# Set attention and a gated convolution: x in two host layouts, float32 scores in column strips, row-tiled gates

## The chip, the cores and the metric

One NeuronCore of one Trainium2 chip. The metric is the device time of one execution in microseconds. TensorE multiplies, VectorE (DVE), ScalarE (ACT) and GpSimd (POOL) work on tiles of 128 partitions, SyncE (SP) issues most DMAs; TensorE's results go to PSUM, eight banks of 128 x 512 float32, which GpSimd does not read.

## The reference

Four batches of 12800 tokens with 128 channels, 32 inducing vectors, five convolution taps, cut to what is computed:

```python
def mab(q, kv):
    s = scale * (q @ kv.transpose(0, 2, 1))
    s = s - s.max(-1, keepdims=True)
    a = np.exp(s)
    a /= a.sum(-1, keepdims=True) + 1e-09
    return a @ kv
h = mab(I, x)                 # 32 rows over 12800 tokens of the batch
x = mab(x, h)                 # 12800 rows over 32
xp = np.concatenate([np.zeros((B, K - 1, D)), x], axis=1)
for k in range(K):
    gate_pre += conv_w[k][None, None, :] * xp[:, k:k + S, :]
gate = 1.0 / (1.0 + np.exp(-gate_pre))
return (gate * (x @ w_val)) @ w_out
```

The second attention's output is never formed: with P the 12800 x 32 softmax, x = P h, so gate and value are products of P with h scaled by each tap, and with h w_val. x comes as float32, the weights as float64 bits that the kernel turns into float32 itself.

## The kernel before

**Layout.** A batch lies as 128 partitions of 100 consecutive tokens. Seven chunks of 8, 12 and 5 x 16 token columns (1024 to 2048 tokens) are the unit; six to eight columns, 512 KB at most, the unit of a load.

**Phase 1 of a batch, `sched_a` and `sched_b`.** `load` brings x on SP's queue. `split1` (L188, ScalarE) and `split2` (L200, VectorE) split it into two float16 halves x1 and x2. These are turned channel-first into xT, by `trans_dma` (L206, L209: a transposing DMA on SP's queue) or, for some chunks of batch 0, by `trans_pe` (L217) and copies out of PSUM. `scores` (L255 to L259) makes the scores of a token column by two or three float16 matmuls with xT as the loaded weight and 32 or 64 moving columns. Then maxima over the chunk (L289 to L302), subtraction on GpSimd (L307), exponential, two float16 halves of it, sums on GpSimd (L334 to L341) and h as float16 products accumulated over the chunk (L355, L356).

**Preparation, `prep0` to `prep8`.** The chunks' h are brought to one maximum and normalised; scaled by the taps and multiplied by w_val they give the weights wst, and w_out scaled gives wo.

**Phase 2, `sched_c` and `sched_phase2`.** `c_mm` scores with h; `c_max` (L486), `c_sub` (L492), `c_exp` (L497), `c_sum` (L505 to L507), `c_norm` (L515), `c_hi` and `c_lo` (L530) give P in two float16 halves, repeated in four groups of 32 columns, p4. A transposing DMA (`y_t`, L544) or TensorE (`y_mm`, L553) turns p4 into y, the four groups on four times 32 partitions, so that one matmul takes several taps or halves together. Two DMAs (L579, L580) write z, y shifted by a tap. For each slot of 4 token columns `f_gate` makes four float16 matmuls of 512 columns on all 128 rows, the last of them with z (five without z), `f_val` one, `f_tanh` (L602) and `f_gv` (L607) gate the value, `f_out` (L613) multiplies each token column by wo in float32 with the gated tile as weight, `f_store` (L619) copies out of PSUM and stores 256 KB on ScalarE's queue.

**Order.** Each step is put at a time in units of the slot by tables of numbers (`AD`, `BS`, `CT`, `F2`, ...), and the events are written out in order of time; a scheduler in the framework may still move instructions. Phase 1 of batch b+1 runs under phase 2 of batch b. PSUM holds two buffers `a`, three `b`, one each for `g`, `v` and `o`.

Of the kernel before, what the change touches and what calls it, by code (L numbers as in the profile page):

```python
# [21 lines left out]
NB = 100  # L22
TAPS = 5
HALO = TAPS - 1
SX = 64.0
SI = 64.0
SE = 4096.0
SH = 64.0
SW = 1024.0
SP = 16384.0  # L30
TINY = 1e-30


@with_exitstack
def tile_kernel(ctx: ExitStack, tc: tile.TileContext, x, inducing, w_val, conv_w, w_out, out):
    nc = tc.nc
    B = x.shape[0]
    SCALE = 1.0 / math.sqrt(P)
    V, S, T, G = nc.vector, nc.scalar, nc.tensor, nc.gpsimd

    xv = x.rearrange("b (p i) c -> b p i c", i=NB)
    ov = out.rearrange("b (p i) c -> b p i c", i=NB)

    chunks = [(0, 8), (8, 12)] + [(20 + 16 * g, 16) for g in range(5)]
    NCK = len(chunks)
# [23 lines left out]
    def copy(e, dst, src):
        if e == "S":  # L70
            S.copy(dst, src)
        else:
            (V if e == "V" else G).tensor_copy(dst, src)  # L73

    anchor = {}

    def pinned(e):
        if PIN and e in anchor:
            return tc.issue_after(anchor[e].ins)
        return contextlib.nullcontext()  # L80

    c_ = {}
    tpn = [0]
    st = {}
    bat = [dict() for _ in range(B)]
    xf_ = {}
    ys = {}
    zs = {}

    def constants():  # L90
# [727 lines left out]
```

## Time and profile before

| | |
|---|---|
| timed runs | 453.2, 459.19, 460.04 us (median 459.19) |
| profiled execution | span 452.9 us from first to last instruction, 11587 instructions; its time around the span is not given apart |
| granted TensorE clock, mean | 0.899 |
| DMA | 137397 packets, 93.18 MB, mean 206 GB/s |
| HBM | 26.50 MB read, 26.21 MB written |
| 0 to 56 us (batch 0's phase 1) | PE busy 36.0, DVE 45.8, ACT 34.7, POOL 33.3, clock 0.74 |
| 430 to 452.9 us (end) | PE busy 17.2, DVE 5.7, ACT 10.8, clock 0.95 |

The page gives busy time by engine, then digits: the span in 40 slices, each digit the busy share in tenths. The chain is followed back from the last instruction to what released each step. A group row reads: line, engine, operation, output tile <- input tiles, shapes, count | busy us, mean ns of one | idle us of the engine before them and who ended it. A row of stretches gives, for a window, busy us and count by engine, then the granted clock, the share of the 16 DMA engines and GB/s. L numbers are lines of the kernel; PEld is the weight load. A float32 matmul of the program appears as two records.

### The profile page before, as it was taken

Reading aid. Unit: us, or ns where it says so; the run is one execution under the profiler, and the core shown is the slowest. Engines: PE = TensorE matmul, PEld = TensorE weight load, DVE = VectorE, ACT = ScalarE, POOL = GpSimd, SP = SyncE. Lnnn points to the kernel's source line nnn. Section 1 sums busy time; section 2 is a strip of 40 time slices with the busy share of each in tenths; the row PEclk is TensorE's granted clock in tenths of the full one; section 3 lists DMA queues with packets and bytes.
Section 4 is the critical chain, followed back from the end, with each engine's and each line's share of the span. In section 5 each row is a group of like instructions: output and inputs, shape, how many; then the busy total and the mean of one; then the engine's idle time right before and its main releaser. Section 6 shows DMA issues by size and latency. Waiting matters only on the chain.

```text
span 452.9 us, 11587 instructions
## 1 busy us (share of the span) xinstructions
PE 355.6 (79%) x4597; PEld 274.8 (61%) x4597; DVE 346.0 (76%) x778; ACT 269.3 (59%) x454; POOL 216.1 (48%) x267
## 2 busy tenths in 40 slices
PE   3677656778899757887598868978779898988795
PEld 3576544557776545666386646756558676755463
DVE  4998899889877757997857878998939998665231
ACT  6667343486667535767555656676756566665353
POOL 2269827465865024584627313594737435462000
PEclk9666655799999988999979997999979999999898
DMA  8999539899999999999999798999997856789853
GB/s 290 255 236 201 112 77 204 205 250 257 240 245 200 171 166 233 242 235 230 203 241 272 187 198 173 289 243 243 229 211 178 172 155 163 158 186 224 178 162 117
DMA packets 137397, 93.18 MB, mean 206 GB/s; under 512 B 114016, under 2 KB 114304, under 8 KB 137344
## 3 DMA queue, kind: packets, MB, share of 16 engines
q1 hardware_dynamic: 121952, 65.94, 73.4%
q10 hardware_dynamic: 15392, 26.50, 17.9%
q8 instruction: 36, 0.59, 0.6%
q14 instruction: 17, 0.14, 0.1%
HBM read 26.50 MB, written 26.21 MB: 116 GB/s over the span
## 4 chain that ended last, share of the span: by engine, by line
DMA 39%; PE 27%; DVE 14%; POOL 7%; ACT 6%; issue 5%; SPq 1%; ACTq 0%; POOLq 0%; DVEq 0%
DMA xT<-x 19%; DMA z<-y 8%; PE g L589 7%; PE o L613 7%; DMA y<-p 6%; DMA out_dram<-os 4%; DVE x L200 2%; DVE g L607 2%; DMA xf<-in_x_dram 2%; PE v L596 2%; PE yp L553 2%; PE s L259 2%; ACT g L602 2%; PE s L255 1%; ACT x L188 1%
## 5 line engine op out<-in xcount | busy, mean ns | idle before, releaser
L613 PEld LDWEIGHTS o<-wo,g 128*128 128x128 f32 x800 | 106.5, 198 | 20.3 <-ACT os L619 7.3
L613 PE MATMUL o<-wo,g 128*128 128x128 f32 x800 | 114.2, 286 | 2.8 <-ACT os L619 1.7
L607 DVE SCALAR_TENSOR_TENSOR g<-g,v 128x512 f32<-128x512 f32 x100 | 67.7, 677 | 44.4 <-ACT g L602 33.6
L602 ACT ACTIVATE g<-g,gsc 128x512 f32<-128x512 f32 x100 | 68.8, 688 | 51.9 <-PE g L589 40.0
L619 ACT COPY os<-o 128x512 f32<-128x512 f32 x100 | 58.6, 586 | 56.2 <-PE o L613 41.7
L589 PE MATMUL g<-y,wst 128*128 128x512 f16 x296 | 83.0, 392 | 1.5 <-ACT g L602 1.5
L200 DVE SCALAR_TENSOR_TENSOR x<-xf,x 128x1024 f16<-128x1024 f32 (+1 forms) x51 | 70.8, 1396 | 1.0 <-ACT x L188 1.0
L589 PEld LDWEIGHTS <-wst 128*128 128x128 f16 x408 | 38.1, 100 | 46.6 <-DMA z<-y 17.5
L259 PEld LDWEIGHTS <-xT 128*128 128x128 f16 x800 | 59.2, 99 | 8.6 <-issue 4.2
L492 POOL TENSOR_TENSOR e<-e,m 128x512 f32<-128x512 f32 (+2 forms) x28 | 29.5, 1054 | 67.2 <-DVE m L486 61.7
L257 PE MATMUL s<-i,xT 128*128 128x32 f16 x356 | 33.9, 181 | 30.0 <-DMA xT<-x 28.9
L515 POOL TENSOR_TENSOR e<-e,z 128x512 f32<-128x512 f32 (+2 forms) x28 | 32.1, 1147 | 49.9 <-DVE z L507 33.2
L188 ACT ACTIVATE x<-xf 128x1024 f16<-128x1024 f32 (+1 forms) x52 | 52.1, 1019 | 5.7 <-DMA xf<-in_x_dram 5.5
L257 PEld LDWEIGHTS <-xT 128*128 128x128 f16 x404 | 33.1, 99 | 34.8 <-DMA xT<-x 32.1
L589 PE MATMUL g<-z,wst 128*128 128x512 f16 x92 | 36.2, 394 | 15.7 <-DMA z<-y 15.7
L530 POOL TENSOR_TENSOR p<-e,p 128x512 f16<-128x512 f32 (+2 forms) x28 | 36.4, 1301 | 19.2 <-DVE p L73 17.3
L596 PE MATMUL v<-y,wst 128*128 128x512 f16 x96 | 37.4, 390 | 6.1 <-DVE g L607 6.0
L307 POOL TENSOR_TENSOR s<-s,mb 128x512 f32<-128x512 f32 (+2 forms) x26 | 34.6, 1332 | 11.9 <-DVE mb L302 11.8
L255 PE MATMUL s<-h,xT 128*128 128x64 f16 x384 | 32.6, 196 | 3.3 <-DVE h L412 3.3
L258 PEld LDWEIGHTS <-xT 128*128 128x128 f16 x404 | 33.0, 99 | 3.0 <-issue 1.2
L259 PE MATMUL s<-i,xT 128*128 128x32 f16 x362 | 33.8, 180 | 0.3 <-DMA xT<-x 0.3
L258 PE MATMUL s<-i,xT 128*128 128x32 f16 x356 | 33.7, 180 | 0.0
(159 smaller groups left out, 763.5 us busy)
## 6 DMA issues: line engine op xcount, KB each, us to landing
out_dram<-os ACTq DMA_DIRECT2D x100, 256.0 KB, 4.0
xf<-in_x_dram SPq DMA_DIRECT2D x40, 512.0 KB, 5.4
z<-y SPq DMA_DIRECT2D x40, 256.0 KB, 4.4
xf<-in_x_dram SPq DMA_DIRECT2D x8, 384.0 KB, 4.5
xf<-in_x_dram SPq DMA_DIRECT2D x8, 256.0 KB, 4.2
z<-y SPq DMA_DIRECT2D x8, 192.0 KB, 4.1
xT<-x SPq DMA_TRANSPOSE x52, 5.8
y<-p SPq DMA_TRANSPOSE x11, 7.5
```

The source lines that it names most:

```text
L188: S.mul(x12[:, 0, :m], xf_[b, c, q][:, :m], SX)
L200: V.scalar_tensor_tensor(x2, xf, SX, x1, ALU.mult, ALU.subtract)
L255: T.matmul(sc[:, i, :], hi, rhs.rearrange("p a j -> p (a j)"), start=True, stop=False)
L257: T.matmul(sc[:, i, :], hi, rhs[:, 1, :], start=True, stop=False)
L258: T.matmul(sc[:, i, :], hi, rhs[:, 0, :], start=False, stop=False)
L259: T.matmul(sc[:, i, :M], lo, rhs[:, 0, :], start=False, stop=True)
L589: T.matmul(gp, d["wst"][:, k, :], r[:, q + o:q + o + 4, :].rearrange("p i t -> p (i t)"), start=i == 0, stop=i == len(taps) - 1)
L596: T.matmul(vp, d["wst"][:, 6, :], y[:, HALO + q:HALO + q + 4, :].rearrange("p i t -> p (i t)"), start=True, stop=True)
L602: anchor["S"] = S.activation(g, st[b, c, q, "g"], AF.Tanh, scale=bat[b]["gsc"])
L607: anchor["V"] = V.scalar_tensor_tensor(g, g, 1.0, st[b, c, q, "v"], ALU.add, ALU.mult)
L613: T.matmul(op[:, i, :], st[b, c, q, "gv"][:, i, :], bat[b]["wo"], start=True, stop=True)
L619: S.copy(os, st[b, c, q, "o"])
```

## The change

Hardly a line of the body stays. What is computed is the same; what differs:

- **Host layouts.** x is passed twice. `xt` is channel-first: a batch is four strips of 3200 consecutive tokens, each with 32 tokens of its predecessor ahead (zeros for strip 0), in blocks of 32 tokens, the four strips side by side. `xk` has, for a block, 4 x 32 tokens on the partitions, 128 channels and a one. Output leaves channel-first and the host transposes it; weights come in one packed array. Batch 0 loads only xt and makes xk by float32 transposes on TensorE (`make_xk`, L302, copies L307 and L309).
- **Scores** (`s1` L326, `s2` L546). Float32, with indT or hT (128 x 32) as weight and 512 tokens moving; the four strips go to PSUM partitions 0, 32, 64 and 96, that is to four groups of 32 columns of the array. VectorE copies s1 with the running maximum in one instruction (L334). Softmax over 32 needs the tokens on partitions: 32 x 32 transposes on VectorE (L398, L552, L589).
- **h** (L412): per 32-token block a float32 matmul of 129 columns (the last sums), strip by strip in the same four column groups; sums over chunks on VectorE. Maxima are shared by groups of chunks (`gmax`).
- **Gate and value** (`gate_mm` L624, `val_mm` L633): P as two float16 halves P1 and P2, strip r on partitions 32r to 32r+31. Gate: 15 matmuls of 32 rows, 128 output columns and 512 tokens for each strip (5 taps x 2 halves, and 5 for the weights' low half); value: 3. `rblock` deals them out row by row over the four strips, two strips half a chunk ahead of the other two. Taps are offsets in P's columns; y and z are gone.
- **Output** (`outp` L706): one float32 matmul, wo as weight, 512 tokens moving, per strip. ScalarE copies (L712), SP stores (L717).
- **Order.** TensorE's order is the order in which the code lists its steps, with `FILL` naming the half chunk under which each step of the next batch goes; `Plan.order` orders the other engines by a list schedule with fixed costs. The framework moves nothing. PSUM: four banks g0 to g3 for the gates, four buffers `a` for all else.

Core of the diff:

```diff
--- before
+++ after
-HALO = TAPS - 1
-SX = 64.0
-SI = 64.0
-SE = 4096.0
-SH = 64.0
+R = 4
+HALO = 32
+SIZES = [128, 512, 512, 512, 512, 512, 512]
+NCK = len(SIZES)
+STRIP = sum(SIZES)
...
-            nc.sync.dma_start_transpose(xT.rearrange("p e i t -> p (e i) t"), x12.rearrange("p e i c -> p (e i c)"))
...
-        nc.sync.dma_start_transpose(dst, p4[:, :n].rearrange("p i s j -> p (i s j)"))
...
-            dma[ZQ[0]].dma_start(z[:64], ys[b, c][:64, 0:n, :])
-            dma[ZQ[1]].dma_start(z[64:], ys[b, c][:64, 1:n + 1, :])
...
+    def load_xt(b, c, early=0.0):
+        n = wid(c)
+        o = R * (first[c] + (HALO if c else 0))
+        key = ("xt", b, c)
+
+        def f():
+            x = sb(pxt, key, [P, n // 32, R, 32], F32, [P, 16, R, 32])
+            nc.sync.dma_start(x.rearrange("p i r q -> p (i r q)"), xt[b, :, o:o + R * n])
+
+        ix[key] = op("SP", n * 2048 / BW, f, [], early, [key])
...
+            def tp(g=g, k=k, tk=tk):
+                t = pt(tk, [P, 4, P])
+                x = st["xt", b, c]
+                for i in range(k):
+                    T.transpose(t[:, i, :], x[:, o + g + i].rearrange("p r q -> p (r q)"), c_["identf"])
...
+    def s1(b, c):
+        n = SIZES[c]
+        o = HALO // 32 if c == 0 else 0
+        key, ss, mx = ("a", "s1", b, c), ("ss", b, c), ("mx", b)
+        new = c == ORD1[b][0]
+
+        def f():
+            s = pt(key)
+            x = st["xt", b, c]
+            for r in range(R):
+                T.matmul(s[32 * r:32 * r + 32, :n], c_["indT"], x[:, o:o + n // 32, r, :], start=True, stop=True)
+
+        i = PE(COST["s"] * n + COST["switch"], f, [ix["xt", b, c], i_ind, i_const], [key], [("xt", b, c)])
+
+        def g():
+            e = sb(pw, ss, [P, 512])
+            if new:
+                sb(pb, mx, [P, NCK])
+            V.tensor_scalar(e[:, :n], st[key][:, :n], 1.0, None, ALU.mult, ALU.max, accum_out=st[mx][:, c:c + 1])
...
+            e = st[ss]
+            S.activation(e[:, :n], e[:, :n], AF.Exp, bias=st["ng", b][:, g:g + 1], scale=SCALE)
...
+        def tr():
+            V.transpose(sb(pw, et, [P, 512])[:, :n], st[ss][:, :n])
...
+        def f():
+            t = pt(key)
+            e, x = st["et", b, c], st["xk", b, c]
+            for i in range(nb):
+                s = i % R
+                T.matmul(t[32 * s:32 * s + 32, :P + 1], e[:, 32 * i:32 * i + 32], x[:, i, :],
+                         start=i < R, stop=i >= nb - R)
...
+        def acc():
+            if c == cs[0]:
+                V.tensor_copy(sb(pb, H, [P, P + 1]), st[key][:, :P + 1])
+            else:
+                V.tensor_tensor(st[H], st[H], st[key][:, :P + 1], ALU.add)
...
+        def f():
+            s = pt(key)
+            x = st["xt", b, c]
+            for r in range(R):
+                T.matmul(s[32 * r:32 * r + 32, :n], st["hT", b], x[:, :, r, :], start=True, stop=True)
...
+        def tin():
+            e = sb(pw, ek, [P, 16, M])
+            V.transpose(e[:, :nb].rearrange("p i j -> p (i j)"), st[key][:, :n])
...
+        def mx():
+            V.tensor_reduce(sb(pw, mk, [P, 16, 1])[:, :nb, 0], st[ek][:, :nb], AX.X, ALU.max)
...
+        def sub():
+            e = st[ek][:, :nb]
+            G.tensor_tensor(e, e, st[mk][:, :nb].broadcast_to([P, nb, M]), ALU.subtract)
...
+        def ex():
+            e = st[ek][:, :nb]
+            S.activation(e, e, AF.Exp, scale=SCALE)
...
+        def tout():
+            q = sb(pw, qk, [P, 512])
+            V.transpose(q[:, :n], st[ek][:, :nb].rearrange("p i j -> p (i j)"))
...
+            S.copy(st[p1][:, o:o + n], st[qk][:, :n])
...
+            G.tensor_tensor(st[p2][:, o:o + n], st[qk][:, :n], st[p1][:, o:o + n], ALU.subtract)
...
+    taps = [(k, e, 0) for k in range(TAPS) for e in range(2)] + [(k, 0, 1) for k in range(TAPS)]
+
+    def gate_mm(b, c, r, u):
+        if u == 0:
+            pt((f"g{r}", b, c))
+        k, e, w = taps[u]
+        n, o = SIZES[c], HALO + first[c] - (TAPS - 1 - k)
+        q = slice(32 * r, 32 * r + 32)
+        T.matmul(st[f"g{r}", b, c][:, :n], st["W", b][q, w, k, :], st[("P1", "P2")[e], b][q, o:o + n],
+                 start=u == 0, stop=u == len(taps) - 1)
+
+    def val_mm(b, c, r, u):
...
+        e, w = ((0, 0), (1, 0), (0, 1))[u]
+        n, o = SIZES[c], HALO + first[c]
+        q = slice(32 * r, 32 * r + 32)
+        T.matmul(st["a", "v", b, c, r][:, :n], st["W", b][q, w, TAPS, :], st[("P1", "P2")[e], b][q, o:o + n],
+                 start=u == 0, stop=u == 2)
...
+        ends, other = ((0, 1), (2, 3)) if half == 0 else ((2, 3), (0, 1))
+        cur = seqs[k] if 0 <= k < len(seqs) else None
+        val = (seqs[k - 1] if k else None) if half == 0 else cur
+        nxt = cur if half == 0 else (seqs[k + 1] if k + 1 < len(seqs) else None)
+        work = {r: [] for r in range(R)}
...
+            for r in ends:
+                work[r] += [(gate_mm, *cur, r, u) for u in range(SPLIT, len(taps))]
...
+            work[r] += [(val_mm, *val, r, u) for u in range(3)] if val else [None] * 3
+            work[r] += [(gate_mm, *nxt, r, u) for u in range(SPLIT)] if nxt else []
...
+        def part(us, new):
+            todo = [[work[r][u] for r in range(R) if u < len(work[r]) and work[r][u]] for u in us]
+
+            def f():
+                for row in todo:
+                    for fn, *a in row:
+                        fn(*a)
...
+        i0 = part(range(3), newv)
+        i = part(range(3, depth), newg)
...
+    def outp(b, c, r):
+        n = SIZES[c]
+        key, os = ("a", "o", b, c, r), ("os", b, c, r)
+
+        def f():
+            T.matmul(pt(key)[:, :n], st["wo", b], st["tg", b, c, r][:, :n], start=True, stop=True)
...
+        def store():
+            nc.sync.dma_start(out[b, :, r, first[c]:first[c] + n], st[os][:, :n])
...
+FILL = [
+    (-4, "s1", 0), (-3, "s1", 1), (-2, "s1", 2), (-1, "gm", 0), (-1, "s1", 3), (0, "gn", 0), (1, "h", 0), (2, "h", 1),
+    (2, "h", 2), (3, "s1", 4), (4, "s1", 5), (5, "s1", 6), (6, "gm", 1), (7, "gn", 1), (8, "h", 3), (8, "h", 4),
+    (9, "h", 5), (9, "h", 6), (10, "prep"), (10, "prep2"), (11, "prep3", 0), (12, "prep3", 1),
+]
+LEAD = 1
+BUFS = dict(xt=10, xk=4, ss=4, et=3, e=3, pt=2, tg=6, os=4, H=4, mx=2, ng=2, m1=2, mr=2, mr4=2, f=2, D=8, Z=8, hT=2,
+            gmx=2, vmx=2, gsc=2, wo=2, w2=2, W=2, P1=2, P2=2, m2=3, z=3, a=4, g0=1, g1=1, g2=1, g3=1)
...
+    xs = x.reshape(B, R, STRIP, C)
+    head = _np.zeros((B, R, HALO, C), x.dtype)
+    head[:, 1:] = xs[:, :-1, STRIP - HALO:]
+    xs = _np.concatenate([head, xs], axis=2)
...
+    xk = _np.ones((B, R, 32, NB, C + 1), x.dtype)
+    xk[..., :C] = x.reshape(B, R, NB, 32, C).transpose(0, 1, 3, 2, 4)
+    xk = xk.reshape(B, R * 32, NB * (C + 1))
...
+    return _np.ascontiguousarray(got.transpose(0, 2, 1))
```

On TensorE, in the middle of a batch, a slot's gate before: four matmuls on all rows, g the PSUM tile, y and z4 the moving tiles, wst the weights.

```order
L589 LDWEIGHTS wst
L589 MATMUL g<-y,wst 128x512
L589 LDWEIGHTS wst
L589 MATMUL g<-y,wst 128x512
L589 LDWEIGHTS wst
L589 MATMUL g<-y,wst 128x512
L589 LDWEIGHTS wst
L589 MATMUL g<-z_5024,wst 128x512
```

And now, inside `rblock` of a chunk of batch 0 (g0 to g3 the strips' PSUM tiles, P1 and P2 the halves of P):

```order
L624 LDWEIGHTS W_675
L624 MATMUL g0_1319<-P1_683,W_675 128x512
L624 LDWEIGHTS W_675
L624 MATMUL g1_1321<-P1_683,W_675 128x512
L624 LDWEIGHTS W_675
L624 MATMUL g2_1243<-P1_683,W_675 128x512
L624 LDWEIGHTS W_675
L624 MATMUL g3_1245<-P1_683,W_675 128x512
```

Four neighbours go to four tiles on disjoint rows, and for 2048 tokens the gate's matmuls go from 16 (20 without z) to 60, the value's from 4 to 12.

On TensorE again, where value and output meet before (v and o PSUM tiles; the gated tile g is the weight of the output product):

```order
L596 LDWEIGHTS wst
L596 MATMUL v<-y,wst 128x512
L613 MATMUL o<-wo,g 128x128
L589 LDWEIGHTS wst
L589 MATMUL g<-z_5220,wst 128x512
L613 MATMUL o<-wo,g 128x128 x3
```

And now, between two `rblock`s, with h of the next batch (xk, et) among the output products (tg, wo):

```order
L412 MATMUL a_1350<-xk_582,et_1317 32x129 x16
L706 MATMUL a_1371<-tg_1275,wo_673 128x512
L412 MATMUL a_1384<-xk_824,et_1369 32x129 x16
L706 MATMUL a_1406<-tg_1279,wo_673 128x512
L624 LDWEIGHTS W_675
L624 MATMUL g0_1319<-P1_683,W_675 128x512
L624 LDWEIGHTS W_675
L624 MATMUL g1_1321<-P1_683,W_675 128x512
L633 LDWEIGHTS W_675
L633 MATMUL a_1418<-P1_683,W_675 128x512
```

Column strips, full array and row strips follow each other within a half chunk, all but the gates through the four buffers `a`.

On SP's queue before, well inside the program:

```order
L206 DMA_TRANSPOSE xT_4892<-x12_4847 128x16x128
L182 DMA xf_4995<-in_x_dram 128x1024
L206 DMA_TRANSPOSE xT_4927<-x12_4908 128x16x128
L579 DMA z4_5024<-y_4914 64x1536
L580 DMA z4_5024<-y_4914 64x1536
L182 DMA xf_5040<-in_x_dram 128x1024
```

And now, where batch 0's first stores are issued:

```order
L277 DMA xk_582<-in_xk_dram 128x2064
L266 DMA xt_612<-in_xt_dram 128x2048
L266 DMA xt_800<-in_xt_dram 128x2048
L277 DMA xk_824<-in_xk_dram 128x2064
L717 DMA out_0_dram<-os_905 128x128
L277 DMA xk_911<-in_xk_dram 128x2064
L717 DMA out_0_dram<-os_932 128x128
```

Only loads and stores remain, all in this one queue, where the stores were on ScalarE's before.

More of the change, by code (lines that the diff above doesn't have):

```diff
@@ L34, in tile_kernel, with cost @@
+def cost(kind, n):
+    a, b = COST[kind]
+    return a + b * n
 @with_exitstack
-def tile_kernel(ctx: ExitStack, tc: tile.TileContext, x, inducing, w_val, conv_w, w_out, out):
+def tile_kernel(ctx: ExitStack, tc: tile.TileContext, xt, xk, indT_in, w64, out):
     nc = tc.nc
-    B = x.shape[0]
-    SCALE = 1.0 / math.sqrt(P)
+    B = xt.shape[0]
     V, S, T, G = nc.vector, nc.scalar, nc.tensor, nc.gpsimd
[L41 to L45, printed above, removed]
@@ L69, in copy, with PE @@
[L69 to L80, printed above, removed]
+    plan = Plan()
+    pe = []
     c_ = {}
-    tpn = [0]
     st = {}
[L85 to L90, printed above, removed]
+    def PE(dur, fn, deps=(), new=(), use=()):
+        i = plan.op("PE", dur, fn, deps, 0.0, new, use)
+        pe.append(i)
+        return i
@@ new lines, in cmax, with sb @@
+        def cmax():
+            c_["wval"], c_["wout"], c_["cwT"] = c_["w"][:, :P], c_["w"][:, P:2 * P], c_["w"][:, 2 * P:]
+            c_["cmax"] = const.tile([P, 1], F32, name="cmax")
+            V.tensor_reduce(c_["cmax"], c_["cwT"], AX.X, ALU.max, apply_absolute_value=True)
+        return op("DVE", 0.1, cmax, [i])
+    first = [0]
+    for n in SIZES:
+        first.append(first[-1] + n)
+    ix = {}
+    def sb(pool, key, shape, dt=F32, pad=None):
+        t = st[key] = pool.tile(shape, dt, name=key[0], tag=key[0], bufs=BUFS[key[0]], padded_shape=pad)
+        return t
@@ new lines, in tile_kernel, with need, S1, Hs @@
+    for c in ORD1[0]:
+        load_xt(0, c)
+    iw = weights(op("SP", 1.0, f_wload))
+    loads = [f for b in range(1, B) for c in ORD1[b] for f in ((load_xt, b, c), (load_xk, b, c))]
+    def need(b, c):
+        while loads and ("xk", b, c) not in ix:
+            f, *a = loads.pop(0)
+            f(*a)
+    def S1(b, c):
+        need(b, c)
+        s1(b, c)
+    def Hs(b, g, c):
+        e1(b, g, c)
+        h(b, g, c)
+    prev = None
+    for g, cs in enumerate(GROUPS[0]):
+        for c in cs:
+            s1(0, c)
+            make_xk(0, c, ("S", "V"))
+        second = gmax(0, g)
+        if prev:
+            for c in GROUPS[0][prev[0]]:
+                Hs(0, prev[0], c)
+        second()
+        prev = (g,)
@@ new lines, in tile_kernel @@
+    for k in range(-1, len(seqs) + 1):
+        for half in range(2):
+            if (k < 0 and not half) or (k == len(seqs) and half):
+                continue
+            rblock(k, half)
+            q = k - 1 if half == 0 else k
+            rs = (2, 3) if half == 0 else (0, 1)
+            fill = slots.get(2 * k + half, [])
+            outs = [(outp, (*seqs[q], r)) for r in rs] if 0 <= q < len(seqs) else []
+            for pair in itertools.zip_longest(fill, outs):
+                for it in pair:
+                    if it:
+                        it[0](*it[1])
```

1061 lines of the change are left out of this document (436 added, 625 removed).

## Prediction

> **What bounds the kernel now.** I read the page's stage digits first, then its chain of waits, then the groups by line, then stretches of 80 to 100 us.
>
> ```profile
> PE 355.6 (79%) x4597; PEld 274.8 (61%) x4597; DVE 346.0 (76%) x778; ACT 269.3 (59%) x454; POOL 216.1 (48%) x267
> ...
> PE   3677656778899757887598868978779898988795
> ...
> DVE  4998899889877757997857878998939998665231
> ...
> DMA  8999539899999999999999798999997856789853
> ...
> DMA 39%; PE 27%; DVE 14%; POOL 7%; ACT 6%; issue 5%; SPq 1%; ACTq 0%; POOLq 0%; DVEq 0%
> DMA xT<-x 19%; DMA z<-y 8%; PE g L589 7%; PE o L613 7%; DMA y<-p 6%; DMA out_dram<-os 4%; DVE x L200 2%; DVE g L607 2%; DMA xf<-in_x_dram 2%; PE v L596 2%; PE yp L553 2%; PE s L259 2%; ACT g L602 2%; PE s L255 1%; ACT x L188 1%
> ```
>
> The DMA engines are full nearly throughout, and the chain lies on them for 39%: the transposes xT and y and the copies z, which only move data about on the chip, are 33 points of that. Loads and stores are 6.
>
> ```profile
> q1 hardware_dynamic: 121952, 65.94, 73.4%
> ...
> 3.00:6.00 3.00, 0.59 (x5) 0.49 (x6) 0.93 (x5) 1.06 (x1) 0.33 (x2) 1.00 1.02 395
> ...
> 140.00:240.00 100.00, 76.70 (x1028) 59.63 (x1028) 74.47 (x166) 58.85 (x101) 44.63 (x55) 0.93 1.07 218
> 240.00:340.00 100.00, 80.04 (x1070) 61.65 (x1067) 80.66 (x177) 62.95 (x110) 52.19 (x64) 0.93 1.03 223
> ```
>
> In mid-program 218 GB/s fill the engines (share over 1); with loads alone (3 to 6 us) they moved 395. SP's queue q1 takes 73% of their time. TensorE and VectorE are 75 to 80% busy there, so neither is far behind: taking the transposes away alone would buy perhaps a fifth. What the change makes of TensorE's work decides.
>
> **What the change does to DMA.** The issues, with their count and the median time to landing:
>
> ```profile
> out_dram<-os ACTq DMA_DIRECT2D x100, 256.0 KB, 4.0
> xf<-in_x_dram SPq DMA_DIRECT2D x40, 512.0 KB, 5.4
> z<-y SPq DMA_DIRECT2D x40, 256.0 KB, 4.4
> ...
> z<-y SPq DMA_DIRECT2D x8, 192.0 KB, 4.1
> xT<-x SPq DMA_TRANSPOSE x52, 5.8
> y<-p SPq DMA_TRANSPOSE x11, 7.5
> ```
>
> All 63 transposes and 48 z copies go. What is left: xt 26.5 MB, xk for three batches 19.8 MB, stores 26.2 MB, 72.5 MB. At 395 GB/s that is 184 us, at the mid-program 223 it would be 325. What is left are plain copies of 2 to 8 KB a partition; the stretch of 395 held plain copies of x, up to 4 KB a partition, and the 223 has the transposes in it. So I take 184: half of the time, no bound. All issues stand in one queue on SP, loads ahead of stores; a load that waits for its buffer holds the stores behind it.
>
> **TensorE: the rates.** The next rows are pieces of the chain (start, us, what) and groups by shape.
>
> ```profile
> 152.30 0.87 PE g L589 x4
> ...
> 164.91 1.71 PE o L613 x8
> ...
> 254.65 0.89 PE o L613 x8
> ...
> L613 PE MATMUL o<-wo,g 128*128 128x128 f32 x800 | 114.2, 286 | 2.8 <-ACT os L619 1.7 <-DVE g L607 1.0
> L613 PEld LDWEIGHTS o<-wo,g 128*128 128x128 f32 x800 | 106.5, 198 | 20.3 <-ACT os L619 7.3 <-ACT g L602 3.0 <-issue 2.3
> L589 PE MATMUL g<-y,wst 128*128 128x512 f16 x296 | 83.0, 392 | 1.5 <-ACT g L602 1.5
> ...
> L299 PE MATMUL t<-dg,ones 32*128 32x32 f32 x42 | 8.9, 293 | 3.0 <-DVE dg L298 3.0
> ```
>
> A float16 matmul of 512 columns takes 0.87/4 = 0.217 us in a row of its like. The 400 float32 output products leave 800 records, two each; a record of 128 columns takes 0.89/8 = 0.111 us (1.71/8 where the clock was halved), so one of 512 takes 0.444 and a whole float32 product of 512 columns 0.89.
>
> New work, at full clock, in records one behind the other:
> - Gate and value: 72 matmuls of 512 columns for each of 24 chunks and 72 of 128 for each of 4: 25 x 72 x 0.217 = 392 us. They stand on four groups of 32 rows, four banks of PSUM.
> - Scores s1 and s2: 25 chunks' worth each, 4 strips, 2 records of 0.444: 2 x 25 x 8 x 0.444 = 178 us. Four groups of 32 columns.
> - h: 400 products of 129 columns, 2 x 0.111 each: 89 us, also in four strips.
> - Output, full array: 25 x 4 x 0.89 = 89 us. Before it was 800 x 0.111 = 89 too.
> - Batch 0's 100 transposes, 11 us at a record each; preparations about 8.
>
> The unknown is whether matmuls in disjoint strips run side by side. No row shows it: L299 uses 32 rows but stands alone. Bounds: one after the other, 392 + 178 + 89 = 659 us; four at a time, 98 + 44.5 + 22 = 165. What speaks for four at a time: a record lasts 392 ns and the next begins after 217, so TensorE never waits for the one before to end, only for the cells it needs; here the cells, the banks and the moving rows are disjoint and nothing orders neighbours. I take a quarter. TensorE's sum is then 98 + 44.5 + 22 + 89 + 19 = 273 us, against 659 + 108 = 767.
>
> The Trainium skill, page "TensorE: Matmul & The Clock Gate", section "Measured speedup vs the span model", gives 3.07 for four row tiles of 512 columns, not 4. By that figure gate and value would be an estimated 128 us and the sum 30 us more. No run here shows it.
>
> **Switches between shapes.** A half chunk goes row strips, column strips, full array, column strips, full array, row strips: some 4 switches, 56 a batch. If the array has to empty, each costs what a lone record lasts beyond its column time, 392 - 217 = 0.17 us: 9.5 us a batch; if not, nothing. In the timeline the old kernel goes from float32 to float16 shapes without a gap, but always on the full array. I take 9.5. The Trainium skill, page "TensorEngine Tiling (Array Packing)", "Key Properties", says that changing the tiling mode drains TensorE. By that rule the switches are paid in full.
>
> **The other engines.** Rows for the operations of the same size:
>
> ```profile
> L607 DVE SCALAR_TENSOR_TENSOR g<-g,v 128x512 f32<-128x512 f32 x100 | 67.7, 677 | 44.4 <-ACT g L602 33.6 <-PE v L596 10.2 <-ACT e L475 0.3
> ...
> L486 DVE TENSOR_REDUCE m<-e 128x16 f32<-128x512 f32 x20 | 13.5, 676 | 0.4 <-ACT e L475 0.3
> ...
> L506 DVE TENSOR_SCALAR z<-z 128x16 f32<-128x16 f32 x20 | 5.0, 252 | 0.1
> ...
> L602 ACT ACTIVATE g<-g,gsc 128x512 f32<-128x512 f32 x100 | 68.8, 688 | 51.9 <-PE g L589 40.0 <-PE v L596 3.3 <-PE s L259 2.4
> ...
> L619 ACT COPY os<-o 128x512 f32<-128x512 f32 x100 | 58.6, 586 | 56.2 <-PE o L613 41.7 <-DMA out_dram<-os 8.2 <-PE h L356 2.2
> ...
> L497 ACT ACTIVATE e<-e 128x512 f32<-128x512 f32 x20 | 12.8, 638 | 4.6 <-POOL e L492 4.2 <-ACT os L619 0.4
> ...
> L530 POOL TENSOR_TENSOR p<-e,p 128x512 f16<-128x512 f32 x20 | 27.5, 1374 | 15.8 <-DVE p L73 15.0 <-DVE z L506 0.8
> ```
>
> VectorE, a chunk of 512: four gate products 2.7; the fused score copy and maximum, two reductions and three 32x32 transposes, 6 x 0.68 = 4.1; small ones 0.25 x 3 = 0.8: 7.6 us. The transposes have no row; between a pass of 0.68 and twice that (2 us a chunk more) I take the pass, since every float32 row of 512 here is near it. With the small chunk, maxima and preparation this is 58 us a batch, 240 in all. ScalarE: 4 x 0.69 + 4 x 0.59 + 3 x 0.64 = 7.0 a chunk, 190. GpSimd: 3 x 1.2 to 1.4, under 100. Before, VectorE had 346 us and ScalarE 269; the float16 splits of x are gone.
>
> **The sum**, in stages. Start to gates of batch 0: first megabyte at 5 us; then 6.25 chunks at the larger of TensorE (0.89 + 16 x 0.111 + 0.89 = 3.6) and VectorE (two copies for xk, maximum, transpose, about 3.6), some 27 with the last group's lag; then the serial preparation. The old one is in the timeline, from the last copy of h to the first transpose of weights:
>
> ```profile
> 56.88 0.21 DVE L367 COPY h<-h 128x64 f32<-128x64 f32 x1
> ...
> 65.98 0.29 PE L451 MATMUL t<-ident,w 128*128 128x128 f16 x1 [1.39 <-DVE w L447]
> ```
>
> 9 us; the new one adds two copies of the weights out of PSUM and, beside them, the first s2 with its softmax: 15 in all, an estimate. That makes 47. Batches 0 to 2: gate and value 24.5, output 22.2, s2 5.6, the next batch's s1 5.6 and h 5.6, preparation 2, switches 9.5, together 75; VectorE's 58 and ScalarE's 47 lie under it, for which I add 5% of waits: 79 each, 236. Last batch without s1 and h: 61, with waits 64. Tail: gate, tanh, product, output, copy, store at 4 us, 8. 47 + 236 + 64 + 8 = 355. The profiled execution's span is 452.9; the three times run from 453.2 to 460.0 with median 459.2, 0 to 7 us above it. With 4 us for that the forecast is **360 us** on the scale of the median. Waits of 15% instead of 5 would make it 390; free switches 320. The rates are those of the full clock; the mid-program rows show 0.93 granted, and half the clock in the first stage would add 15 us at most. Its own range is 325 to 395.
>
> **Rivals.**
> *Strips start in order, so float32 strips only half overlap* (0.30). Each float32 product is two records on the same strip. If a record that must wait for its own strip holds all behind it, the second record of strip 0 runs beside the first of strip 1, and so on: 5 steps of 0.444 for a score instead of 2 (2.22 us against 0.89), 17 of 0.111 for h instead of 8. That adds 25 x (2 x 1.33 + 1.0) = 91 us, of which the waits I added and VectorE's time in stage one absorb some 10: **440 us**. For it: 800 records for 400 products. Against: TensorE already takes up what comes later while a record runs, a weight load of 198 ns for each record of 111. The float16 rows are dealt out strip by strip and would not suffer. The Trainium skill, page "TensorE: Matmul & The Clock Gate", section "The mechanism", has matmuls start and end strictly in program order, which speaks for this rival; this trace has no case.
>
> *The PSUM ring binds* (0.12). Eleven products a chunk (4 value, 4 output, s2, s1, h) share four buffers in turn. At 12.6 us a chunk a buffer may be held 4.6 us; a value buffer waits for two tanh and two VectorE products, about 3. If queues on VectorE, 75% busy, stretch it to 5.5: 11 x 5.5 / 4 = 15 us a chunk, 25 x 2.5 = 63 more: **420 us**.
>
> *Row strips do not run side by side* (0.13). Then gate and value cost 392 in place of 98: 360 + 294 = **654 us**, slower. The turn is at 360 + 99 = 459: a row of four (450 of them) taking 0.22 us more, 0.44, i.e. two at a time. Against it: separate banks for each strip, and that nothing in the rows makes one wait.
>
> **How the numbers follow.** 0.45 for the forecast. The range must reach into 440 and 420; 325 to 455 holds nearly all of the forecast, most of the ring and four fifths of the ordered strips, 0.78 or so. A measurement of this kernel tells 2% from no change (450 to 468 is "same"). Faster: 0.45 + 0.11 + two thirds of 0.30, 0.76; same 0.09; slower 0.15.
>
> **What would show it.** Right: no transposes on a queue, DMA under 0.6 of its engines; four gate records with starts a few ns apart and rows 0.22 us apart; a score's eight records in 0.9 us, h of a chunk in 0.9; TensorE the largest share of the chain and a granted clock near 1 from 50 us on. A score in 2.2 us is the first rival; TensorE waiting for ScalarE's os or VectorE's tg is the second; gate rows of 0.87 us the third. Wrong altogether if the gates of batch 0 begin after 65 us, or SP's stores hold ScalarE.

## The result and the profile after

The new kernel takes **352.87 us** (median of 4 runs, 352.03 to 354.31), beside 458.31 (453.2 to 460.04) for the kernel before: a ratio of 0.7722, 95% interval 0.766 to 0.7784. Forecast were 360 us, range 325 to 455. Ratios, here and below, leave out executions that took over 1.5% longer than the fastest of the same kernel, so they are not quite those of the medians. The span of the profiled execution is 351.2 us, the mean granted clock 0.971.

The page, in the order in which it was read before: busy time, digits, DMA queue, chain by engine and by line.

```profile
PE 326.2 (93%) x3868; PEld 139.3 (40%) x3868; DVE 231.2 (66%) x577; ACT 182.2 (52%) x331; POOL 86.1 (25%) x107
...
PE   3899657987999999999999999999999999999994
...
PEclk9999855999999999999999999999999999999999
DMA  8981950775459936994679645982222332223333
...
q1 hardware_dynamic: 23472, 72.80, 55.8%
...
PE 84%; DVE 7%; DMA 5%; ACT 1%; issue 1%; POOL 0%; SPq 0%; ACTq 0%; DVEq 0%
PE a L706 28%; PE g L624 23%; PE a L326 8%; PE a L412 7%; PE a L546 6%; PE a L633 6%; PE g L302 4%; DMA xt<-in_xt_dram 4%; DMA indT<-in_indT_dram 1%; DVE tg L696 1%; PE a L520 1%; PE a L356 1%; PE a L373 1%; DVE pt L589 1%; DVE z L575 1%
```

The chain has moved from DMA (39% before) to TensorE (84%). The PE row is nines from the eleventh slice (88 us) to the end, the DMA row mostly not. Cut at the first gate matmul of each batch, the stages are these (busy us and count by engine, then clock, DMA share, GB/s):

```profile
0.00:47.00 47.00, 35.23 (x454) 24.25 (x454) 32.87 (x110) 15.00 (x26) 2.64 (x17) 0.94 0.75 299
47.00:62.00 15.00, 11.07 (x106) 4.26 (x110) 6.69 (x21) 3.38 (x7) 3.86 (x6) 0.50 0.14 58
62.00:134.00 72.00, 67.80 (x840) 26.70 (x829) 48.98 (x123) 36.75 (x67) 18.85 (x21) 1.00 0.70 251
134.00:211.00 77.00, 76.75 (x950) 30.42 (x950) 55.20 (x136) 43.45 (x80) 21.11 (x23) 1.00 0.73 261
211.00:283.00 72.00, 71.78 (x905) 29.36 (x900) 51.60 (x124) 41.99 (x78) 20.52 (x23) 1.00 0.45 168
283.00:341.00 58.00, 57.93 (x618) 22.54 (x612) 33.55 (x63) 38.11 (x69) 19.08 (x18) 1.00 0.31 117
```

From 134 us TensorE is busy 76.75 of 77, 71.78 of 72 and 57.93 of 58 us: nothing else matters there. All that it loses to others lies ahead of that, in batch 0, and so does half a clock from 47 to 62. The stages against the forecast:

| stage (first gate matmul to the next) | forecast | measured |
|---|---|---|
| start to batch 0 | 47 | 49.0 |
| batches 0, 1, 2 | 79 each | 85.7, 76.6, 72.2 |
| last batch, to its last gate matmul | 64 | 58.1 |
| tail | 8 | 9.6 |
| span | 355 | 351.2 |

Batches 0 to 2 differ for one plain reason among others: seven chunks of s1 belong to the next batch, and `FILL` runs some of them before the batch's first gate. Batch 0's stage holds eleven of these steps, batch 1's seven, batch 2's three.

A piece of TensorE's timeline in batch 1 (start, us, line, shapes, count):

```profile
156.86 0.39 PE L624 MATMUL g<-P,W 32*128 32x512 f16 x2
156.86 0.39 PE L633 MATMUL a<-P,W 32*128 32x512 f16 x2
157.08 0.38 PE L624 MATMUL g<-P,W 32*128 32x512 f16 x2
157.09 0.38 PE L633 MATMUL a<-P,W 32*128 32x512 f16 x2
157.30 0.38 PE L624 MATMUL g<-P,W 32*128 32x512 f16 x2
157.31 0.38 PE L633 MATMUL a<-P,W 32*128 32x512 f16 x2
157.52 1.47 PE L624 MATMUL g<-P,W 32*128 32x512 f16 x24
158.91 1.07 PE L546 MATMUL a<-xt,hT 128*32 128x512 f32 x8
159.91 1.13 PE L706 MATMUL a<-tg,wo 128*128 128x512 f32 x2
160.96 1.07 PE L326 MATMUL a<-xt,indT 128*32 128x512 f32 x8
161.96 1.12 PE L706 MATMUL a<-tg,wo 128*128 128x512 f32 x2
```

Four matmuls, two of gate and two of value, start within some 10 ns, the next four 0.22 us later. Six rows of four (24 records) are followed after 158.91 - 157.52 = 1.39 us by a score, and the score's eight float32 records, two for each strip, by the next shape after 1.00 us. One after the other they would be 24 x 0.217 = 5.2 and 8 x 0.427 = 3.4 us. In the records of that score the first ones of all four strips start at 158.912 to 158.932, the second ones 0.427 us later. Strips do run side by side, four at a time, in float32 as in float16.

### The profile page after: what moved, and what is told of

Same layout as the page of the kernel before. It is cut to its first block, busy times and chain, and to the rows that moved or that the text cites. A ratio compares the mean times of both kernels' runs of the same rounds, so it can differ in the third digit from the quotient of the medians.

```text
span 351.2 us, 9468 instructions
## 1 busy us (share of the span) xinstructions
PE 326.2 (93%) x3868; PEld 139.3 (40%) x3868; DVE 231.2 (66%) x577; ACT 182.2 (52%) x331; POOL 86.1 (25%) x107
## 3 DMA queue, kind: packets, MB, share of 16 engines
q1 hardware_dynamic: 23472, 72.80, 55.8%
## 4 chain that ended last, share of the span: by engine, by line
PE 84%; DVE 7%; DMA 5%; ACT 1%; issue 1%; POOL 0%; SPq 0%; ACTq 0%; DVEq 0%
PE a L706 28%; PE g L624 23%; PE a L326 8%; PE a L412 7%; PE a L546 6%; PE a L633 6%; PE g L302 4%; DMA xt<-in_xt_dram 4%; DMA indT<-in_indT_dram 1%; DVE tg L696 1%; PE a L520 1%; PE a L356 1%; PE a L373 1%; DVE pt L589 1%; DVE z L575 1%
## 5 line engine op out<-in xcount | busy, mean ns | idle before, releaser
L624 PE MATMUL g<-P,W 32*128 32x512 f16 (+1 forms) x1680 | 115.1, 354 | 3.4 <-POOL P L610 3.4
L706 PE MATMUL a<-tg,wo 128*128 128x512 f32 (+1 forms) x224 | 108.8, 586 | 0.9 <-DVE tg L696 0.9
L685 ACT ACTIVATE tg<-g,gsc 128x512 f32<-128x512 f32 (+1 forms) x112 | 67.5, 639 | 58.3 <-PE g L624 58.0
L712 ACT COPY os<-a 128x512 f32<-128x512 f32 (+1 forms) x112 | 60.4, 541 | 55.8 <-PE a L706 42.7
L696 DVE SCALAR_TENSOR_TENSOR tg<-tg,a 128x512 f32<-128x512 f32 (+1 forms) x112 | 65.2, 619 | 31.3 <-PE a L633 28.1
L624 PEld LDWEIGHTS <-W 32*128 32x128 f16 x1680 | 48.1, 93 | 57.6 <-issue 19.2
L706 PEld LDWEIGHTS a<-tg,wo 128*128 128x128 f32 x224 | 35.2, 188 | 51.7 <-issue 20.5
L633 PE MATMUL a<-P,W 32*128 32x512 f16 (+1 forms) x336 | 43.3, 356 | 0.1
L604 POOL TENSOR_TENSOR P<-pt,P 128x512 f16<-128x512 f32 (+1 forms) x28 | 29.8, 1063 | 52.8 <-ACT P L597 52.8
L326 PE MATMUL a<-xt,indT 128*32 128x512 f32 (+1 forms) x224 | 30.8, 629 | 9.7 <-DMA indT<-in_indT_dram 5.7
L552 DVE STREAM_TRANSPOSE e<-a 128x512 f32<-128x512 f32 (+1 forms) x28 | 18.5, 660 | 18.6 <-PE a L546 18.5
L546 PE MATMUL a<-xt,hT 128*32 128x512 f32 (+1 forms) x224 | 29.0, 592 | 1.0 <-DVE hT L468 1.0
L412 PE MATMUL a<-xk,et 128*32 128x129 f32 x800 | 27.7, 277 | 1.7 <-DVE D L443 1.2
L334 DVE TENSOR_SCALAR_CACHE_REDUCE ss<-a 128x512 f32<-128x512 f32 (+1 forms) x28 | 17.6, 630 | 16.3 <-PE a L326 16.3
L412 PEld LDWEIGHTS a<-xk,et 128*32 128x32 f32 x800 | 21.0, 110 | 14.6 <-issue 7.3
L589 DVE STREAM_TRANSPOSE pt<-e 128x512 f32<-128x512 f32 (+1 forms) x28 | 18.3, 655 | 11.1 <-POOL e L583 11.1
L597 ACT CAST P<-pt 128x512 f16<-128x512 f32 (+1 forms) x28 | 16.1, 575 | 13.3 <-DVE pt L589 12.9
```

Source lines behind the costliest of these rows:

```text
L326: T.matmul(s[32 * r:32 * r + 32, :n], c_["indT"], x[:, o:o + n // 32, r, :], start=True, stop=True)
L412: T.matmul(t[32 * s:32 * s + 32, :P + 1], e[:, 32 * i:32 * i + 32], x[:, i, :], start=i < R, stop=i >= nb - R)
L546: T.matmul(s[32 * r:32 * r + 32, :n], st["hT", b], x[:, :, r, :], start=True, stop=True)
L604: G.tensor_tensor(st[p2][:, o:o + n], st[qk][:, :n], st[p1][:, o:o + n], ALU.subtract)
L624: T.matmul(st[f"g{r}", b, c][:, :n], st["W", b][q, w, k, :], st[("P1", "P2")[e], b][q, o:o + n], start=u == 0, stop=u == len(taps) - 1)
L633: T.matmul(st["a", "v", b, c, r][:, :n], st["W", b][q, w, TAPS, :], st[("P1", "P2")[e], b][q, o:o + n], start=u == 0, stop=u == 2)
```

## Experiments

The first question is why four strips fill so well. **Theory A:** a matmul whose strip is busy waits without holding those behind it, if only a few wait. **Its rival** is the prediction's: a matmul that must wait holds all that come later. The score above speaks for A, since each strip's second record stands directly behind its first. But is it the order by hand that makes the time, and how many may wait? The second question is what TensorE still loses: shape changes, the ring of four PSUM buffers, loads, clock. The runs' times are medians; the kernel before, on the same chips, had 458.93 (first four), 458.84 (next four) and 455.06 us (last three).

**Two matmuls of a strip in a row.** In `rblock`:

```diff
-                for row in todo:
-                    for fn, *a in row:
-                        fn(*a)
+                for j in range(0, len(us), 2):
+                    for r in range(R):
+                        for u in us[j:j + 2]:
+                            if u < len(work[r]) and work[r][u]:
+                                fn, *a = work[r][u]
+                                fn(*a)
```

> Only the order of the gate and value matmuls inside a part is changed: two for strip 0, two for strip 1, and so on, instead of one for each strip in turn. Theory A, each row strip takes its matmuls from a queue of its own, so one that waits for its strip lets the next strip's pass: nothing changes, 350 to 357 us, rows of four still 0.217 us apart on average. Theory B, matmuls start strictly in the order of the program: two rows take 4 steps of 0.217 instead of 2, the 97 us of gate and value double, about 450 us.

Measured: 356.19 us. Stages: 50.9, then 86.3, 76.7, 72.3 and 58.3. Batches 1 to 3 differ by 0.1 to 0.2 us from the changed kernel's; 1.9 of the 3.3 us lie before the first gate. The half chunk after the one shown above, in this kernel's timeline:

```profile
165.55 0.39 PE L633 MATMUL a<-P,W 32*128 32x512 f16 x2
165.56 0.39 PE L624 MATMUL g<-P,W 32*128 32x512 f16 x2
165.77 0.38 PE L633 MATMUL a<-P,W 32*128 32x512 f16 x2
165.79 0.38 PE L624 MATMUL g<-P,W 32*128 32x512 f16 x2
165.99 0.38 PE L633 MATMUL a<-P,W 32*128 32x512 f16 x2
166.00 1.68 PE L624 MATMUL g<-P,W 32*128 32x512 f16 x26
```

In program order two of a strip stand together; in time there are still four strips to a row, 0.22 us apart. One waiting matmul holds nothing. The strict order is out.

**All matmuls of a strip in a row** (three in the first part of a half chunk, six in the second):

```diff
-                for row in todo:
-                    for fn, *a in row:
-                        fn(*a)
+                for r in range(R):
+                    for u in us:
+                        if u < len(work[r]) and work[r][u]:
+                            fn, *a = work[r][u]
+                            fn(*a)
```

> As the run with pairs, but all matmuls of a strip in a part (3 or 6) stand together. Theory A with a deep queue: 350 to 360 us. Theory B, strictly in order: only the last of a strip and the first of the next overlap, 9 and 21 steps of 0.217 instead of 3 and 6, 3.3 times the 97 us: about 580 us. A queue that looks ahead only a few matmuls lies between, nearer to 580.

Measured: 413.2 us, 60 more. Its timeline, and two pieces of its chain:

```profile
165.49 0.39 PE L633 MATMUL a<-P,W 32*128 32x512 f16 x2
165.51 0.40 PE L624 MATMUL g<-P,W 32*128 32x512 f16 x2
165.72 0.38 PE L633 MATMUL a<-P,W 32*128 32x512 f16 x2
165.74 0.38 PE L624 MATMUL g<-P,W 32*128 32x512 f16 x2
165.93 0.38 PE L633 MATMUL a<-P,W 32*128 32x512 f16 x2
165.95 3.01 PE L624 MATMUL g<-P,W 32*128 32x512 f16 x26
```

```profile
172.65 2.62 PE g L624 x24
...
185.78 2.62 PE g L624 x24
```

With three of a strip together the four strips still start within 30 ns. With six, 24 records take 2.62 us, and 1.30 in the same pieces of the changed kernel's chain: 12 steps of 0.217 in place of 6. That is what follows if a strip has one matmul running and three waiting, and a fourth holds everything behind it: strip 0's last enters the wait when its third starts, so each strip begins two steps after its neighbour, and 3 x 2 + 6 = 12. With two waiting it would be 15 steps, with four 9. Nor do all strips share three places: with three of each strip in a row up to eight matmuls wait, and still nothing is held. Over 48 half chunks of 512 columns 6 x 0.217 us make 62, measured 60. A batch has twelve of them, 15.6 us; batches 1 to 3 are 15.4, 15.8 and 16.1 us longer.

**h with the blocks of a strip in a row**, the same question in float32:

```diff
-            for i in range(nb):
+            for i in [R * j + s for s in range(R) for j in range(nb // R)]:
```

> Only h is reordered: the four (or one) blocks of a strip stand together instead of going round the four strips; the same sums. Theory A: no change, 350 to 357 us. Theory B: the 32 records of a chunk take 29 steps of 0.107 us instead of 8, 2.3 us more for each of 25 chunks, 56 us, some of it hidden in the first stage: about 400 us.

Measured: 383.37 us, 30.5 more. A chunk of h in its chain, and in that of the changed kernel:

```profile
108.93 2.41 PE a L412 x32
```

```profile
98.32 1.02 PE a L412 x32
...
108.65 1.06 PE a L412 x32
```

A strip has eight records here (four products of two). With three waiting, each strip begins four steps behind its neighbour: 3 x 4 + 8 = 20 steps instead of 8, and 12 x 0.111 = 1.33 us; measured 2.41 - 1.04 = 1.37. Six chunks of 512 columns make 8.2 us a batch; batches 1 and 2 are 8.3 us longer, and the last, which runs no h, not at all. The depth of three fits both kinds. So the order by hand matters only beyond a depth that this kernel never reaches.

**Fewer gate rows.** Is TensorE's row the price of time? Gate's five products with the low halves of the weights are left out, 14 rows for 18, SPLIT 4 for 6:

```diff
-    taps = [(k, e, 0) for k in range(TAPS) for e in range(2)] + [(k, 0, 1) for k in range(TAPS)]
+    taps = [(k, e, 0) for k in range(TAPS) for e in range(2)]
...
-    SPLIT = 6
+    SPLIT = 4
```

> Leaves out the gate's products with the low float16 halves of the weights (5 of 15) and splits the other ten 4 and 6 over the two half chunks, so a chunk has 14 rows of four matmuls instead of 18. If TensorE's time is what bounds phase 2: 4 x 0.217 x 25 = 21 us less, 330 to 334 us. If VectorE or ScalarE or the four shared PSUM buffers bind it: less than 10 us, 343 or more.

Measured: 337.73 us, 15 less, between the two forecasts. The batches are 3.9, 4.3, 4.1 and 4.5 us shorter; four rows of 0.217 us for each of 6.25 chunks are 5.4. The waits for the gated tile, which the changed kernel had once, in the tail:

```profile
PE a L706 <- DVE tg L696: 4.1, 8, 1.0
```

TensorE's idle time is 1.9 to 2.3 us in each later batch. So its rows set most of the time, and the engines behind it are near: the missing us of each batch went into new waits.

**One PSUM buffer fewer**, the ring that was a rival:

```diff
-            ... m2=3, z=3, a=4, g0=1, g1=1, g2=1, g3=1)
+            ... m2=3, z=3, a=3, g0=1, g1=1, g2=1, g3=1)
```

> Three shared PSUM buffers instead of four for all but the gates. If the ring was near its limit (the rival of the prediction: a buffer may be held 4 x 11.4 / 11 = 4.1 us at the 11.4 us that a chunk takes), three allow 3.1 us and TensorE waits for ScalarE's copies and VectorE's products: 380 to 440 us. If there was slack: under 365 us.

Measured: 363.06 us (ratio 0.7903), 10 more; 7.7 of it in batch 0, 1.0 and 1.9 in the next two, none in the last. From batch 1 on TensorE is still idle for 0.2 to 1.3 us a batch only, and in batch 0 for 8.0 instead of 6.1, again at loads of xt. The clock lost more: 22.8 us of batch 0 ran at half of it, 13.1 in the changed kernel, and with TensorE busy in nearly all of the difference that is some 5 of the 7.7 us. TensorE waited for ScalarE's copies hardly at all (0.2 us in batch 0). The ring of four had slack.

**Fewer shape changes.** The half chunk lists the next batch's steps and the outputs in turn; here all of the one, then all of the other, 188 changes of shape for 233 by the order of the steps (in the traces 43 to 59 fewer, by how matmuls of a single row or column are counted):

```diff
-            for pair in itertools.zip_longest(fill, outs):
-                for it in pair:
-                    if it:
-                        it[0](*it[1])
+            for it in fill + outs:
+                it[0](*it[1])
```

> Between two gate blocks the scores and h come first, then the output products, instead of by turns. The program then has 188 changes of the array's shape instead of 233 and enters the float32 output 18 times less. If a change costs what the trace of the changed kernel shows (0.095 us of emptying, and 0.107 us more for the weight load ahead of the output): 45 x 0.095 + 18 x 0.107 = 6 us less, 346 to 348 us. If the output products, now later, hold the shared PSUM buffers: the gain is eaten by waits of TensorE, 352 us or more.

Measured: 352.92 us (0.7678, 0.7637 to 0.772): nothing. A row of the timeline where it was lost, and a row of its waits:

```profile
82.89 1.93 PE L326 MATMUL a<-xt,indT 128*32 128x512 f32 x8 [3.64 <-DMA xt<-in_xt_dram]
```

```profile
PE a L476 <- DVE hT L468: 3.0, 3, 1.0
```

TensorE came sooner to a load of xt that came no sooner, and waited 3.64 us; behind that the score took 1.93 us in place of 1.07, half the clock until 88.8. In all, 23.0 us of batch 0 ran at half clock, 13.1 in the changed kernel. Batch 0 is 2.2 us longer, the next two 0.6 and 1.6 shorter, each with a new wait for the transposed h, three times 1.0.

**Stores on ScalarE's queue:**

```diff
-            nc.sync.dma_start(out[b, :, r, first[c]:first[c] + n], st[os][:, :n])
+            nc.scalar.dma_start(out[b, :, r, first[c]:first[c] + n], st[os][:, :n])
```

> Stores are issued from ScalarE's queue instead of SP's, nothing else. Theory: batch 0's phase 2 takes 85.7 us against 76.6 of batch 1 because loads of batch 1 stand behind stores in SP's queue (TensorE waits 13 us in all for xt); then some 5 to 8 us less, 345 to 348 us. Rival: the loads are late because the first h of batch 1 frees their buffers late, whatever queue they are in; or 112 issues of 0.34 us on ScalarE cost as much as they bring: 351 to 356 us.

Measured: 352.81 us (0.7679, 0.7627 to 0.7732): nothing either. Why it was tried, in SP's queue of the changed kernel (start, us in the queue) and, for the two loads of xt that come late, on TensorE:

```profile
61.89 0.33 SPq L277 DMA_DIRECT2D xk<-in_xk_dram  x1
...
67.14 0.63 SPq L266 DMA_DIRECT2D xt<-in_xt_dram  x1
...
70.46 8.55 SPq L717 DMA_DIRECT2D out_dram<-os  x4
79.11 0.41 SPq L266 DMA_DIRECT2D xt<-in_xt_dram  x1
```

```profile
75.01 1.07 PE L326 MATMUL a<-xt,indT 128*32 128x512 f32 x8 [1.66 <-DMA xt<-in_xt_dram]
...
84.39 1.07 PE L326 MATMUL a<-xt,indT 128*32 128x512 f32 x8 [2.29 <-DMA xt<-in_xt_dram]
```

The queue stands until 61.89 at an xk that waits for its buffer, then four stores that wait for ScalarE's copies keep the load of 79.11 back. With the stores away, one wait is left of the two:

```profile
72.71 1.07 PE L326 MATMUL a<-xt,indT 128*32 128x512 f32 x8 [0.24 <-DMA xt<-in_xt_dram]
```

and batch 0 takes 83.5 us for 85.7. But the start was 1.7 us longer in this execution, and the later batches 0.2 to 0.8.

**Both together:**

> Both edits, the grouped order and the stores on ScalarE's queue. If each gain is real and they lie in different places (changes of shape throughout, load waits in batch 0), they add: 338 to 343 us. If the first takes up waits that the second removes, less: 345 us or more.

Measured: 345.28 us (0.7536, 0.7479 to 0.7592), 7.6 less. Against the stores alone, batches 0 to 2 are 2.8, 3.2 and 0.8 us shorter. 45 changes at the price worked out below (0.09 us, and 0.11 more for the 18 of them that go from scores or h into an output) make 6. Grouping was worth about what the changes cost, as long as no load stood in its way; alone it was eaten by the load.

**Both, with the next batch's product of h and w_val behind the outputs** (`late` holds `prep2`), against the three waits for hT:

```diff
+            late = [it for it in fill if it[0] is prep2]
+            for it in [it for it in fill if it[0] is not prep2] + outs + late:
+                it[0](*it[1])
```

> As the run with both edits, but the one step of preparation that waited 1 us for VectorE in each of three batches (the product of h with w_val) goes behind the output products instead of ahead of them. Expected: these three waits go, and with them the half-clock stretch of 3.4 us that followed one of them: 3 to 5 us less than with both edits, 341 to 343 us. If the wait only moves on to the weights' transposes behind it: 345 us.

Measured: 343.29 us (0.7535, 0.7492 to 0.7577), 2 us less by the medians, the same by the ratios. By the profiles, batch 2, which with both lost clock at 257.9 us behind one of these waits, takes 69.9 for 72.2; the others change by 0.4 at most.

**Idle work for the clock.** 4, 4 and 12 constant float32 products, into the gates' banks, in the waits of batch 0's preparation (before `s2(0, 0)`, before `prep3(0, 0)`, after `prep3(0, 1)`):

```diff
+            for i in range(n):
+                T.matmul(t[:, :P], c_["identf"], c_["identf"], start=True, stop=True)
...
+    warm(0, 4)
...
+    warm(1, 4)
...
+    warm(2, 12)
```

> The changed kernel with 4, 4 and 12 float32 matmuls of constants, 0.22 us each at full clock, put where TensorE waits in batch 0's preparation (0.99, 0.98 and 3.44 us); their result is never read. Theory: the idle stretches there halve the granted clock from 41.6 to 62.1 us, and 10 us of work at half clock cost 5. With the gaps filled the clock stays up: gates of batch 0 begin at 48 to 50 us as before, its phase 2 takes 4 to 6 us less, 347 to 349 us. Rival: the clock is halved all the same, the fillers run at 0.44 us and push the first gates back by 2 to 4 us: 354 to 357 us.

Measured, in the kernel otherwise unchanged: 351.51 us (0.7728, 0.7691 to 0.7765). The same stretch of this kernel and of the one without:

```profile
49.00:62.00 13.00, 10.25 (x168) 4.74 (x161) 8.70 (x27) 3.69 (x10) 3.25 (x3) 0.87 0.19 58
```

```profile
49.00:62.00 13.00, 11.07 (x106) 4.16 (x109) 6.48 (x20) 2.75 (x7) 2.21 (x3) 0.50 0.01 5
```

The clock is 0.87 instead of 0.50 and 62 records more of the kernel's own work are through (the idle products lie ahead of this stretch, and batch 0 begins 0.7 us earlier), but the time is only 1.4 us less by the medians and no less by the ratios. TensorE then waits for the maximum (2.6 us for 1.9) and for the same loads of xt, 3.8 us in all, and the clock is halved once more, from 80.6 to 84.0 us.

**All of these:** stores on ScalarE's queue, grouped, split, with idle work.

> The run before with the fillers as well. If the two are independent: another 3 to 5 us less, 337 to 340 us; if the clock comes up by itself as early as it did with both edits (59.9 us), only 1 to 2 less.

Measured: 340.82 us (0.7497, 0.7455 to 0.754), the fastest version that leaves nothing out: 12 us below the changed kernel, 2.9% by the two ratios to the kernel before. The idle work makes 2.5 us of that by the medians, between the two forecasts, and the intervals of the ratios with and without it overlap.

## Why the prediction was right

The mechanism was right by its own steps, and the sum came out 4 us over the span, with terms that missed in both directions: by up to 7 us a stage. That they cancel so nearly is luck.

- **Bound and DMA.** DMA is no bound, as said: q1 holds 55.8% of the engines' time, 196 us, where I took 184. The mean hides 0.70 to 0.73 in batches 0 and 1, at 251 to 261 GB/s, which would be some 360 with full engines, not the 395 of the first loads. Nothing hung on that.
- **Side by side.** A quarter of the serial time was right for all three kinds. The rows 0.217 us, h at 1.02 (0.9 said), a score 1.00 to the next shape (0.89 said).
- **Against the page.** The Trainium skill, page "TensorE: Matmul & The Clock Gate", gives 3.07 for four row tiles ("Measured speedup vs the span model"); here 24 records took 1.30 us, six times the 0.217 that one takes in a row of its like, so 4.0. That matmuls start strictly in program order (the Trainium skill, same page, "The mechanism") does not hold here up to three waiting matmuls a strip. The measurement decides in both.
- **Switches.** I counted 4 x 56 = 224 and took 0.17 us each; the program has 233 by the order of its steps. The price was mis-sized. In the chain, four output records in one piece and two in a piece of their own:

```profile
155.01 1.92 PE a L706 x4
...
159.98 1.06 PE a L706 x2
```

  Two pieces of two are 2 x 1.06 - 1.92 = 0.20 us longer than one of four, and this holds two things. A bare change costs some 0.09 us: from a score's last record to the next shape 0.522 us pass instead of 0.427, behind a gate row 0.302 instead of 0.215. The output's first record lasts 697 ns, and the later ones 592, some 0.105 more, which I had not thought of. The likely cause is its weights (128 x 128, in float32), which load while nothing runs: of the two loads of such a pair the second starts 0.108 us after the first, and a score's first records, whose weights have a quarter of the columns, last 617 ns, 25 longer than its others. In batch 1 the matmuls' own time, by count and by the time of their columns, is an estimated 64 to 65.5 of the 76.6 us; the other 11 to 12.6 stand beside the 9.5 of the sum: near in size, other in kind. The Trainium skill, page "TensorEngine Tiling (Array Packing)", "Key Properties", has a change of tiling mode drain TensorE; the trace agrees in that a change costs time, at about half of the price that I gave it.
- **Waits.** 5%, 4 us a batch, was the step that failed: idle TensorE is 0.2 us each in batches 1 and 2, and 6.1 in batch 0, for the two loads of xt and the maximum at half clock. The later load stands behind waiting stores in SP's queue; I had named only stores behind a waiting load, and put no price on it. Of the 9.1 us by which batch 0 is longer than batch 1 the idle time makes 5.9. The work itself is by the counts some 1.5 us less: four more steps of s1 (three of 512 columns and one of 128, 3.5 us), but eight output records (48 for 56) and four and a half rows of gate and value fewer (4.0 and 1.0). What is left, 4.7, fits the clock: TensorE was busy 11.2 us of this batch at half of it, which is about 5.6 too many.
- **Last batch.** 58.1 for 64: without the next batch's steps the switches are fewer too, 34 stays in a shape. I had charged it the full 9.5, and 3 of waits.
- **Other engines.** VectorE 231 us (240 said), ScalarE 182 (190), GpSimd 86 (under 100). The 32 x 32 transposes, which had no row, take one pass and no more:

```profile
L552 DVE STREAM_TRANSPOSE e<-a 128x512 f32<-128x512 f32 x24 | 17.1, 713 | 17.9 <-PE a L546 17.8
L589 DVE STREAM_TRANSPOSE pt<-e 128x512 f32<-128x512 f32 x24 | 17.0, 708 | 11.1 <-POOL e L583 11.1
L398 DVE STREAM_TRANSPOSE et<-ss 128x512 f32<-128x512 f32 x24 | 16.4, 689 | 0.1
```

- **Clock.** Near 1 from 50 us on was wrong by 12 us, and by the account above its price is some 5 us. The idle work won back 1.4 at most: 6.8 us of batch 0 still ran at half clock, and TensorE was idle for 6.8 us instead of 6.1, since it got to the next wait sooner.
- **The rivals.** *Strict order*: its premise failed at the first waiting matmul, and holds at the fourth. Its 440 us are for a depth of none, which no run shows; 413 and 383 are what orders without regard for a depth of three cost. *The ring*: even one buffer fewer costs 10 us, about half of it clock, not the 60 feared with four; the buffers are held less long than I thought. *No side by side*: each row shows otherwise.

What stays open: why the time from the start to the first gate lies anywhere from 48.5 to 50.9 us among kernels that do not differ there. It goes with the half clock ahead of that gate, 7.4 to 9.1 us where the start took 49.0 or less and 11.4 to 12.2 where it took 50.6 or more; but with the idle work it was 48.3 with none and 51.4 with 6.8, so the cause is not shown. So the single changes of queue and order, 0 each and 7.6 together, are shown as sums, and their split by stage only as far as one profile of each goes.

## What to carry to other kernels

Matmuls on disjoint strips can be listed in any order that puts no more than three behind the running one of a strip; check the 0.217 us rows, not the list. Once TensorE is at 99%, count how often the shape of its tiles changes and what weight load each entry exposes, and group by shape, but look first what it will wait for next: a saving ahead of a late load is handed back, with clock lost on top. A load should not stand in one queue behind stores that wait for the end of the pipeline.

## What the runs showed that I had not expected

- A strip holds three waiting matmuls beside the running one, in float16 and in float32: 12 steps for 6 (2.62 us for 1.30) and 20 for 8 (2.41 for 1.04).
- Entering a float32 product with 128 x 128 weights from another shape costs 0.09 us for the change and some 0.105 more in its first record.
- Behind waits as short as 1.0 to 3.6 us the granted clock fell to a half for 3.4 to 6.8 us (82.0 to 88.8 grouped, 3.4 us at 257.9 with both), and in the first preparation for 20.5 us, from 41.6 to 62.1. The length of a wait does not decide it alone: the changed kernel's own waits of 1.66 and 2.29 us for xt left the clock at 1.0.
- A copy of 128 numbers on a single partition (L367) took VectorE 172 to 215 ns five times and 562 to 1101 ns five times. The five slow ones each ran beside a pass of GpSimd and ended 74 to 76 ns after it; the quick ones had none beside them. So a small copy can last as long as GpSimd's pass:

```profile
166.46 1.05 POOL L583 TENSOR_TENSOR e<-e,z 128x512 f32<-128x512 f32 x1 [3.79 <-ACT tg L685]
166.48 1.10 DVE L367 COPY mr<-mr 1x128 f32<-1x128 f32 x1
```
